# Low key rows of the scores: a transfer from the rounded rows in place of a cast on Vector

## The chip, the cores and the metric

The kernel runs on one core of one Trainium2 chip. Its engines are TensorE (PE, with its weight loads shown apart as PEld), VectorE (DVE), ScalarE (ACT), GpSimd (POOL) and SyncE (SP), which here only issues transfers. The metric is the device time of one execution in microseconds. Three runs of the kernel before took 872.01, 875.14 and 871.11 us, a median of 872.01.

## The reference, cut to what matters

Causal attention with a forget bias, then a channel mix; batch 8, 8 heads, 576 positions, head size 64, model width 512, hidden width 1024.

```python
scores = scale * np.matmul(q, k.transpose(0, 1, 3, 2))
cum = np.cumsum(np.maximum(s, 0.0), axis=-1)
bias = -(cum[:, :, :, None] - cum[:, :, None, :])
scores = np.where(causal, -1e9, scores + np.minimum(bias, 0.0))
attn = softmax(scores)
x = (attn @ v)                       # heads side by side: B, S, 512
x_prev = x shifted by one position
xk = mu_k * x + (1 - mu_k) * x_prev
xr = mu_r * x + (1 - mu_r) * x_prev
k = np.maximum(xk @ w_k, 0.0)
out = sigmoid(xr @ w_r) * (k * k @ w_v)
```

## The kernel before

Attention goes in 36 visits, each of one batch and one pair of heads; a visit of batch 0 covers part of the query tiles (three tiles, later the other two), a visit of batches 1 to 7 all five. After the output of enough positions is there, a chunk of 256 positions goes through the channel mix (18 chunks: hidden layer L1184, gate L1226, output L1251). The work of chunks is laid between the visits, and the last chunks stand alone at the end.

Products of two float32 matrices are made of rounded halves (the type fp32r, which TensorE reads in one pass): high part times high part, and so on. For the scores of the last 32 visits, `split_qk` prepares this, head by head (j = 0, 1, so 64 times). The raw keys of a pair lie in `raw`, head 0 on partitions 0 to 63 and head 1 on 64 to 127. ACT rounds the own half into `KH` (L693). POOL subtracts, and writes what rounding left into the other half of `KH` (L697). ACT rounds the queries into `G` (L708), POOL writes their rest into `QL` (L712). A score is then two matmuls into one PSUM bank (L761): `KH` with `G` over 128 rows, and `KL` with `QL` over 67 rows. Rows 0 to 63 of `KL` are the rounded keys once more, on low partitions for both heads; rows 64 to 66 are three parts of the prefix sums, which a small transfer brings (L687). Before the change, rows 0 to 63 were written by a cast on DVE (L703) from the same raw keys. `KH`, `KL`, `G` and `QL` have three buffers each.

The order on every engine is written by a planner (`Plan`). Each operation is added as a task with an engine, a duration from a formula, its readers and writers, and a due time. The planner runs a list schedule forward with these durations, derives new due times backward, does this 20 times and emits the order that ended first by its own reckoning. A task's `quarters` (the partitions of input and output) make an engine 20 ns later when they differ from those of the task before. So a task that changes its engine or its formula changes the order of everything. Every engine works through its list in order; SP issues transfers one after the other, and one whose source or target isn't ready holds those behind it.

Operations that matter here: on DVE the reduction of scores with the mask (L779), the rest of the turned weights `pl` (L889), which the matmuls with the values wait for (L1019), the channel mix's `xp` (L1130), `xl` (L1156), squares (L1206) and `kl` (L1213); on ACT the exponentials (L797) and the casts `ph` (L885); on POOL the normalization (L813) and the rest of the values (L632); on SP the loads of queries (L658), keys (L645), values (L621) and of a chunk's positions `x` (L1276).

Of the kernel before, what the change touches and what calls it, by code (L numbers as in the profile page):

```python
# [29 lines left out]
def f32(ap):  # L30
    return ap.bitcast(F32)
# [281 lines left out]
def forgetting_attention_then_channel_mix(  # L313
# [16 lines left out]
    nc = tc.nc  # L330

    B, H, D, S = q.shape
# [20 lines left out]
    def sbuf(shape, tag, bufs=1, dtype=F32):  # L353
        return plan.buffer(sb, shape, dtype, tag, bufs)
# [15 lines left out]
    def at_quarters(i, quarters):  # L370
        if quarters != (0, 0):
            plan.quarters[i] = quarters
        return i

    def act(emit, reads, writes, n, extra=51, table=0, quarters=(0, 0)):
        return at_quarters(
            plan.add("ACT", n * 0.8333 + extra, emit, reads, writes, land=table), quarters
        )

    def dve(emit, reads, writes, n, rate=0.96, extra=70, quarters=(0, 0)):  # L380
        return at_quarters(plan.add("DVE", n / rate + extra, emit, reads, writes), quarters)

    def pool(emit, reads, writes, n, extra, rate=0.8333, quarters=(0, 0)):
        return at_quarters(plan.add("POOL", n * rate + extra, emit, reads, writes), quarters)

    def dma(emit, reads, writes, ns):
        return plan.add("SP", 1.286 * ns, emit, reads, writes, land=1300)
# [279 lines left out]
    def ahead(emit, what, n):  # L667
        due, plan.due = plan.due, -2.0e5
        dve(emit, [], [what], n)
        plan.due = due  # L670

    def split_qk(b, hp, qs, k):

        nq, nk = qs[0].n, k.n
        found = []
        for j in range(2):
            own, other = slice(64 * j, 64 * j + 64), slice(64 - 64 * j, P - 64 * j)  # L680
            QQ, K = (sbuf([P, n], x, 3, F32R) for n, x in ((nq, "G"), (nk, "KH")))
            QL, KB = (sbuf([P, S], x, 3, F32R) for x in ("QL", "KL"))
            if made[0] < 3:
                made[0] += 1
                ahead(lambda QL=QL: nc.vector.memset(f32(QL.get()[64:67]), 1.0), (QL, 1), S)
            dma(
                lambda j=j, KB=KB: nc.sync.dma_start(  # L687
                    f32(KB.get()[64:67, 0:nk]), cum3_d.ap[b * H + 2 * hp + j, :, 0:nk]
                ),
                [(cum3_d, i) for i in range(3)], [(KB, 1)], 40,  # L690
            )
            act(
                lambda own=own, K=K: nc.scalar.copy(K.get()[own], k.get()[own]),  # L693
                [(k, j)], [(K, j)], nk, 90,
            )
            pool(
                lambda own=own, other=other, K=K: nc.gpsimd.tensor_tensor(  # L697
                    out=K.get()[other], in0=k.get()[own], in1=f32(K.get()[own]), op=ALU.subtract
                ),
                [(k, j), (K, j)], [(K, 1 - j)], nk, 210, 2.21, (2 * j, 2 - 2 * j),  # L700
            )
            dve(
                lambda own=own, KB=KB: nc.vector.tensor_copy(KB.get()[0:64, 0:nk], k.get()[own]),  # L703
                [(k, j)], [(KB, 0)], nk, 1.92, 150, (2 * j, 0),
            )
            x = qs[j]
            act(
                lambda x=x, QQ=QQ: nc.scalar.copy(QQ.get(), x.get()),  # L708
                [(x, 0), (x, 1)], [(QQ, 0), (QQ, 1)], nq, 90,
            )  # L710
            pool(
                lambda x=x, QQ=QQ, QL=QL: nc.gpsimd.tensor_tensor(  # L712
                    out=QL.get()[0:64, 0:nq], in0=x.get()[0:64], in1=f32(QQ.get()[0:64]),
                    op=ALU.subtract,
                ),
                [(x, 0), (QQ, 0)], [(QL, 0)], nq, 210, 2.21,
            )
            found.append(((QQ, K, P), (QL, KB, 67)))
        return found
# [632 lines left out]
    def prepare(n):  # L1352
        qs, ks = loaded.pop(n)
        b, hp, tiles = visits[n]
        vn = load_values(b, hp, -(-KN[tiles[-1]] // P), n < PLAIN)
        QKs[n] = [[(x, ks)] for x in qs] if n < PLAINQ else split_qk(b, hp, qs, ks)
        Vs[n] = vn if n < PLAIN else split_v(vn, vn.n // P)
# [119 lines left out]
```

## Time and profile before

| | |
|---|---|
| median of three runs | 872.01 us |
| the profiled execution, its own time | 871.47 us |
| its span | 869.7 us |
| granted TensorE clock | full (0.999 of 2.4 GHz) |
| busy: PE, DVE, ACT, POOL | 851.7, 698.5, 688.4, 449.5 us |

Busy PE counts a matmul from its start to the modelled end, and neighbours overlap, so a busy share of 98% does not say that TensorE streams without pause. The chain of waits follows the work that ended last back from the end; it says which engine was waited for, and there PE has 76%.

### The profile page before, as it was taken

The numbers are of one execution on the slowest core, as the hardware profiler recorded it, in microseconds if no ns is written. First come the engines' busy times: TensorE is split into PE (matmuls) and PEld (weight loads), VectorE is DVE, ScalarE is ACT, GpSimd is POOL, SyncE is SP. The second block draws the span as 40 slices with busy tenths as digits, with TensorE's granted clock in tenths as the row PEclk, the third lists the DMA queues.
The fourth block names the chain that finished last, engine by engine and source line by source line (L and its number), as shares of the span: only waits on it lengthen the run. The fifth ranks groups of instructions, "written<-read, shape, count | busy, mean of one in ns | idle before, by whom it ended". The sixth has DMA issues, their size and how long they took to land.

```text
span 869.7 us, 17512 instructions
## 1 busy us (share of the span) xinstructions
PE 851.7 (98%) x5519; PEld 751.0 (86%) x5519; DVE 698.5 (80%) x2143; ACT 688.4 (79%) x1854; POOL 449.5 (52%) x719
## 2 busy tenths in 40 slices
PE   9999999999999999999999999999999999999998
PEld 8778789789888888989898988898988889888986
DVE  8999789889888998789878888888888888555431
ACT  6999999999978987898979787988887978445331
POOL 5877887884754665455646545445653642000000
PEclk9999999999999999999999999999999999999999
DMA  8775233251332323223322313132412110100100
GB/s 248 254 233 154 86 115 109 85 153 47 109 117 67 120 64 110 67 83 93 89 88 72 109 55 120 58 104 72 122 55 92 44 62 16 57 22 34 49 25 24
DMA packets 48125, 80.10 MB, mean 92 GB/s; under 512 B 8160, under 2 KB 21472, under 8 KB 48032
## 3 DMA queue, kind: packets, MB, share of 16 engines
q1 hardware_dynamic: 48032, 78.99, 29.7%
q8 instruction: 43, 0.70, 0.3%
q14 instruction: 50, 0.41, 0.2%
HBM read 59.64 MB, written 19.33 MB: 91 GB/s over the span
## 4 chain that ended last, share of the span: by engine, by line
PE 76%; DVE 12%; ACT 8%; issue 3%; DMA 1%; SPq 0%; POOL 0%; ACTq 0%; DVEq 0%
PE m L1251 16%; PE m L1184 16%; PE m L1226 9%; PE s L761 8%; PE po L1019 7%; PE t L856 7%; DVE W L779 3%; ACT W L797 3%; DVE KL L703 2%; DVE pl L889 2%; PE t L1251 2%; PE po L1005 2%; PE s L1184 2%; PE t L1184 2%; PE s L750 1%
## 5 line engine op out<-in xcount | busy, mean ns | idle before, releaser
L1184 PE MATMUL m<-xh,w_k 128*128 128x256 f32 x976 | 205.5, 288 | 0.5 <-ACT xh L1152 0.3
L797 ACT ACTIVATE W<-W,nm 64x64 f32<-64x64 f32 (+4 forms) x320 | 179.6, 562 | 26.3 <-DVE nm L779 22.0
L1251 PE MATMUL m<-w_v,kh 128*128 128x512 f32 x528 | 187.6, 406 | 0.0
L813 POOL TENSOR_SCALAR W<-W,rinv 128x192 f32<-128x192 f32 (+4 forms) x320 | 166.7, 540 | 25.4 <-DVE rinv L839 23.8
L1184 PEld LDWEIGHTS m<-xh,w_k 128*128 128x128 f32 x976 | 160.2, 189 | 3.0 <-ACT xh L1152 0.7
L779 DVE CUSTOM_DVE_ANT_0 W<-s,lower 128x448 f32<-128x448 f32 (+5 forms) x320 | 130.1, 414 | 26.2 <-PE s L761 21.0
L1184 PE MATMUL m<-xl,w_k 128*128 128x256 f32 x488 | 138.9, 285 | 0.0
L856 PE MATMUL t<-ident,W 128*128 128x128 f32 (+1 forms) x736 | 134.0, 275 | 4.5 <-DVE xT L1057 1.8
L697 POOL TENSOR_TENSOR KH<-raw,KH 64x576 fp32r<-64x576 f32 x64 | 92.9, 1451 | 83.9 <-ACT KH L693 45.5
L889 DVE TENSOR_TENSOR pl<-t,ph 128x512 fp32r<-128x512 f32 x224 | 106.4, 484 | 11.9 <-ACT ph L885 9.9
L856 PEld LDWEIGHTS t<-ident,W 128*128 128x128 f32 (+1 forms) x736 | 89.5, 137 | 25.7 <-DVE xT L1057 2.8
L1251 PEld LDWEIGHTS m<-w_v,kh 128*128 128x128 f32 x528 | 97.9, 189 | 14.3 <-ACT g L1238 0.3
L761 PE MATMUL s<-KH,G 128*64 128x64 f32 (+1 forms) x360 | 108.7, 309 | 0.5 <-DVE nm L779 0.5
L885 ACT CAST ph<-t 128x512 fp32r<-128x512 f32 x224 | 93.2, 424 | 17.4 <-PE t L856 14.6
L761 PE MATMUL s<-KL,QL 67*64 67x64 f32 (+1 forms) x360 | 106.1, 299 | 0.0
L1251 PE MATMUL m<-w_v,kl 128*128 128x512 f32 x264 | 106.0, 402 | 0.0
L1130 DVE SCALAR_TENSOR_TENSOR xp<-x,mu,xp 128x256 f32<-128x256 f32 (+3 forms) x184 | 76.3, 415 | 26.5 <-ACT xp L1123 24.1
L1226 PE MATMUL m<-w_r,xh 128*128 128x512 f32 x264 | 95.1, 406 | 0.5 <-DVE kl L1213 0.5
L1123 ACT ACTIVATE xp<-x,mu 128x256 f32<-128x256 f32 (+3 forms) x184 | 77.6, 422 | 22.3 <-DMA x<-x_d 11.7
L712 POOL TENSOR_TENSOR QL<-raw,G 64x576 fp32r<-64x576 f32 (+1 forms) x64 | 86.6, 1353 | 13.3 <-ACT G L708 11.2
L1184 PEld LDWEIGHTS m<-xl,w_k 128*128 128x128 f32 x488 | 92.4, 189 | 0.9
L632 POOL TENSOR_TENSOR V<-vn,V 128x320 fp32r<-128x320 f32 x56 | 48.4, 882 | 70.9 <-ACT V L628 64.5
(161 smaller groups left out, 1899.6 us busy)
## 6 DMA issues: line engine op xcount, KB each, us to landing
raw<-in_q SPq DMA_DIRECT2D x112, 144.0 KB
raw<-in_k SPq DMA_DIRECT2D x32, 288.0 KB
out<-g SPq DMA_DIRECT2D x36, 256.0 KB
vn<-in_v SPq DMA_DIRECT2D x28, 320.0 KB
x_d<-xT SPq DMA_DIRECT2D x28, 288.5 KB
x<-x_d SPq DMA_DIRECT2D x11, 514.0 KB
w_k<-in_moe_w_k SPq DMA_DIRECT2D x8, 512.0 KB
w_v<-in_moe_w_v SPq DMA_DIRECT2D x8, 512.0 KB
```

The costliest lines, as they stand in the source:

```text
L697: lambda own=own, other=other, K=K: nc.gpsimd.tensor_tensor(out=K.get()[other], in0=k.get()[own], in1=f32(K.get()[own]), op=ALU.subtract),
L712: lambda x=x, QQ=QQ, QL=QL: nc.gpsimd.tensor_tensor(out=QL.get()[0:64, 0:nq], in0=x.get()[0:64], in1=f32(QQ.get()[0:64]), op=ALU.subtract,),
L761: lambda x=x, G=G, K=K, n=n: nc.tensor.matmul(ps.get()[:m, :w], G.get()[:n, q0 : q0 + m], K.get()[:n, k0 : k0 + w], start=x == 0, stop=x == 1,
L779: lambda a=a, e=e, to=to, i=i: nc.vector.tensor_tensor_reduce(out=W.ap[:m, to : to + e - a], in0=ps.get()[:m, a - k0 : e - k0], in1=lower. ...
L797: lambda: nc.scalar.activation(W.ap[:m, :n], W.ap[:m, :n], AF.Exp, bias=nm.get()[:m, 3 * t + mi : 3 * t + mi + 1], scale=-1.0, accum_out=s ...
L813: lambda: nc.gpsimd.tensor_scalar(out=to.ap[:m, c : c + n], in0=W.ap[:m, :n], scalar1=rinv.get()[:m, t : t + 1], scalar2=1.0, op0=ALU.mult ...
L856: lambda: nc.tensor.transpose(ps.get()[0:m, place : place + P], pt[t].ap[:, k0 + front(t, tiles) : k0 + front(t, tiles) + m], ident.ap,),
L885: act(lambda: nc.scalar.copy(strips(ph), src()), [ps], [(ph, k) for k in ks], n * m)
L889: lambda: nc.vector.tensor_tensor(out=strips(pl), in0=src(), in1=f32(strips(ph)), op=ALU.subtract),
L1184: lambda u=u, f=f, c=c, n=n, w=w, x=x: nc.tensor.matmul(ps.get()[:, u * CT : (u + 1) * CT], weight["k", c, f // 4].get()[:, w, f % 4 * P : ...
L1226: lambda c=c, n=n, x=x, w=w: nc.tensor.matmul(ps.get(), x.get()[:, c, ts], weight["r", c, 0].get()[:, w], start=c == 0 and n == 0, stop=c ...
L1251: lambda f=f, n=n, x=x, w=w: nc.tensor.matmul(ps.get(), x.get()[:, f, ts], weight["v", f, 0].get()[:, w], start=f == 0 and n == 0, stop=f ...
```

## The change

The cast on DVE of rows 0 to 63 of `KL` is taken out. A transfer on SP's queue writes them, from the own half of `KH`, once ACT has rounded it. The values are the same. The ACT cast's task also tells the planner its partitions now (`quarters`). Nothing else differs, but the planner's order does. Lines behind the change move down by two.

```diff
             act(
                 lambda own=own, K=K: nc.scalar.copy(K.get()[own], k.get()[own]),
-                [(k, j)], [(K, j)], nk, 90,
+                [(k, j)], [(K, j)], nk, 90, quarters=(2 * j, 2 * j),
             )
...
-            dve(
-                lambda own=own, KB=KB: nc.vector.tensor_copy(KB.get()[0:64, 0:nk], k.get()[own]),
-                [(k, j)], [(KB, 0)], nk, 1.92, 150, (2 * j, 0),
+            dma(
+                lambda own=own, K=K, KB=KB: nc.sync.dma_start(
+                    f32(KB.get()[0:64, 0:nk]), f32(K.get()[own])
+                ),
+                [(K, j)], [(KB, 0)], 410 * nk / S,
             )
```

What stands on DVE of the kernel before around the 35th of the 64 casts (a name's number tells its buffer apart; `W` and `nm` are scores and their maxima):

```order
L1130 SCALAR_TENSOR_TENSOR xp_307<-x_164,mu_75,xp_307 128x256
L779 ISA W_71,nm_229<-s_143,lower 64x64
L779 ISA nm_229 64x1
L703 CAST KL_633<-raw_389 64x576
L889 TENSOR_TENSOR pl<-t_316,ph_1439 128x384
L889 TENSOR_TENSOR pl<-t_310,ph_1439 128x256
L1156 TENSOR_TENSOR xl_897<-xp_307,xh_882 128x512
L889 TENSOR_TENSOR pl<-t_310,ph_1439 128x128
L839 RECIPROCAL rinv_313<-rinv_313 128x5
```

And on DVE of the changed kernel at the same scores:

```order
L1132 SCALAR_TENSOR_TENSOR xp_309<-x_164,mu_75,xp_309 128x256
L891 TENSOR_TENSOR pl<-t_315,ph_1436 128x384
L781 ISA W_71,nm_229<-s_143,lower 64x64
L781 ISA nm_229 64x1
L1132 SCALAR_TENSOR_TENSOR xp_309<-x_164,mu_75,xp_309 128x256
L891 TENSOR_TENSOR pl<-t_307,ph_1436 128x256
L841 RECIPROCAL rinv_312<-rinv_312 128x5
L1158 TENSOR_TENSOR xl_926<-xp_309,xh_915 128x512
L891 TENSOR_TENSOR pl<-t_307,ph_1436 128x128
```

The cast that stood ahead of two writes of `pl` is gone, and the first `pl` stands ahead of the reduction.

SP's queue in the kernel before, from the load of a chunk's positions in the third batch on:

```order
L1276 DMA x_164<-x_d_79 128x4x193
L687 DMA KL_569<-cum_d 3x576
L658 DMA raw_433<-in_q 64x576 x2
L658 DMA raw_357<-in_q 64x576 x2
L621 DMA vn_100<-in_v 128x640
L1268 DMA out<-g_1208 128x512
L645 DMA raw_94<-in_k 128x576
L687 DMA KL_633<-cum_d 3x576
```

And in the changed kernel from the same load:

```order
L1278 DMA x_164<-x_d_79 128x4x193
L658 DMA raw_401<-in_q 64x576 x2
L687 DMA KL_527<-cum_d 3x576
L1270 DMA out<-g_1129 128x512
L703 DMA KL_661<-KH_680 64x576
L658 DMA raw_428<-in_q 64x576 x2
L687 DMA KL_585<-cum_d 3x576
L1399 DMA x_d_80<-xT_195 128x577
L621 DMA vn_100<-in_v 128x640
L703 DMA KL_527<-KH_532 64x576
```

Each head has one more entry (L703) between the loads, and the loads behind it issue after it.

## Rows read from the trace of the kernel before

**Rows 1.** The page: busy shares, and the chain of waits by engine and line.

```profile
PE 851.7 (98%) x5519; PEld 751.0 (86%) x5519; DVE 698.5 (80%) x2143; ACT 688.4 (79%) x1854; POOL 449.5 (52%) x719
...
PE 76%; DVE 12%; ACT 8%; issue 3%; DMA 1%; SPq 0%; POOL 0%; ACTq 0%; DVEq 0%
PE m L1251 16%; PE m L1184 16%; PE m L1226 9%; PE s L761 8%; PE po L1019 7%; PE t L856 7%; DVE W L779 3%; ACT W L797 3%; DVE KL L703 2%; DVE pl L889 2%; PE t L1251 2%; PE po L1005 2%; PE s L1184 2%; PE t L1184 2%; PE s L750 1%
```

**Rows 2.** Busy time by stage: stretch, its length, each engine, clock, DMA share.

```profile
0.00:50.00 50.00, 45.26 (x318) 38.45 (x319) 46.38 (x129) 41.95 (x132) 37.77 (x84) 1.00 0.81 245
50.00:250.00 200.00, 194.39 (x1268) 168.42 (x1268) 181.24 (x532) 187.77 (x506) 154.13 (x227) 1.00 0.39 120
250.00:700.00 450.00, 446.06 (x2933) 397.59 (x2931) 381.06 (x1273) 379.56 (x1035) 244.69 (x382) 1.00 0.28 84
750.00:869.70 119.70, 115.97 (x687) 101.83 (x685) 49.63 (x86) 43.37 (x84) 0.00 (x0) 0.99 0.10 33
```

**Rows 3.** The chain of waits by line, of 50 to 250, then 250 to 700.

```profile
by line: PE m L1184 11.4%; PE t L856 8.4%; PE s L761 7.3%; ACT W L797 6.7%; issue 6.5%; PE m L1251 6.4%; PE m L1226 5.5%; PE po L1005 5.0%; DVE W L779 4.6%; DVE KL L703 4.6%; DVE pl L889 3.9%; PE po L1019 3.9%; ACT xp L1123 3.3%; ACT ph L88
...
by line: PE m L1184 20.3%; PE m L1251 18.2%; PE m L1226 11.3%; PE s L761 11.0%; PE po L1019 10.2%; PE t L856 7.2%; DVE W L779 3.0%; DVE KL L703 2.3%; DVE pl L889 2.1%; issue 2.0%; ACT W L797 1.5%; PE t L956 1.3%; PE t L1019 1.2%; DVE pl L94
```

**Rows 4.** Groups by form, the cast: count, busy us, mean ns, idle before.

```profile
L703 DVE CAST KL<-raw 64x576 fp32r<-64x576 f32 x64 | 50.1, 784 | 1.0
```

**Rows 5.** Single lines: minimum, median, maximum ns, first and last start.

```profile
L703 DVE CAST KL<-raw x64: 417/518/2062, 33.5 to 698.3; 64x576 fp32r<-64x576 f32 x64
...
L697 POOL TENSOR_TENSOR KH<-raw,KH x64: 1405/1428/1708, 32.6 to 695.2; 64x576 fp32r<-64x576 f32 x64
```

**Rows 6.** Timeline, a cast with POOL idle (start, us, instruction).

```profile
59.94 0.46 DVE L703 CAST KL<-raw 64x576 fp32r<-64x576 f32 x1
...
60.49 1.41 POOL L697 TENSOR_TENSOR KH<-raw,KH 64x576 fp32r<-64x576 f32 x1 [1.04 <-issue]
```

**Rows 7.** Timeline from 339 to 343, a cast with POOL at work.

```profile
339.55 1.71 POOL L632 TENSOR_TENSOR V<-vn,V 128x320 fp32r<-128x320 f32 x2 [6.13 <-ACT V L628]
...
340.55 1.02 DVE L703 CAST KL<-raw 64x576 fp32r<-64x576 f32 x1
...
341.34 1.52 POOL L697 TENSOR_TENSOR KH<-raw,KH 64x576 fp32r<-64x576 f32 x1
...
341.50 0.97 DVE L889 TENSOR_TENSOR pl<-t,ph 128x384 fp32r<-128x384 f32 x2
...
342.09 0.13 PEld L1019 LDWEIGHTS po<-pl,V 128*64 128x64 f32 x1 [0.46 <-DVE pl L889]
```

**Rows 8.** Timeline, the rounding of keys and their head's first score.

```profile
156.70 0.67 ACT L693 CAST KH<-raw 64x576 fp32r<-64x576 f32 x1
...
161.76 0.24 PE L761 MATMUL s<-KH,G 128*64 128x64 f32 x1
...
694.37 0.67 ACT L693 CAST KH<-raw 64x576 fp32r<-64x576 f32 x1
...
722.79 0.22 PE L761 MATMUL s<-KH,G 128*64 128x64 f32 x1
```

**Rows 9.** The chain in order of time: a transfer of keys at the start.

```profile
3.66 4.36 DMA KH<-in_k
```

**Rows 10.** Waits: who waited for whom, us in total, times, longest.

```profile
SPq L687 <- PE s L761: 141.9, 44, 10.6
...
ACT xp L1123 <- DMA x<-x_d: 11.7, 6, 4.8
```

**Rows 11.** SP's issues by line: minimum, median, maximum ns, first and last start.

```profile
L658 SPq DMA_DIRECT2D raw<-in_q x128: 465/476/1580, 14.4 to 661.4; - x128
...
L1276 SPq DMA_DIRECT2D x<-x_d x23: 529/564/582, 107.0 to 803.8; - x23
```

**Rows 12.** The page: the DMA queue's packets, MB, share of 16 engines.

```profile
q1 hardware_dynamic: 48032, 78.99, 29.7%
```

## The prediction

> **What bounds the kernel now.** I read four views: the page for the engines and the chain of waits, then busy time by stage, then the chain of the two middle stages, then single instructions around the cast.
>
> The page shows PE at 98% and DVE and ACT near 80% [rows 1]. Busy PE includes overlaps, so I go by the chain: 76% PE, 12% DVE, 8% ACT. So for about a fifth of the span TensorE waits for something DVE or ACT has not finished. The cast, L703, has 2% of the chain by itself, about 17 us.
>
> By stage [rows 2] there are three cases. Up to 50 us the DMA engines are 0.81 busy with the first weights. From 50 to 250 us DVE is busy 181.24 of 200 and ACT 187.77, so both are nearly full and PE waits for both. From 250 to 700 us DVE has 381.06 and ACT 379.56 of 450, and PE is close to its own pace. From 750 us on TensorE works alone on the last chunks, POOL does nothing, and no cast is left (the last starts at 698.3 [rows 5]). The clock is full throughout, so it is no term.
>
> In the chain of the stages [rows 3] the cast has 4.6% of the 200 us, which is 9.2 us, and 2.3% of the 450 us, which is 10.35 us: 19.6 us together, against 17 by the page's rounded share.
>
> **What a cast costs.** The 64 casts are busy 50.1 us, 784 ns each in the mean [rows 4], but 417 at least, 518 in the middle and 2062 at most [rows 5]. Their form is one and the same, so something else stretches them. With POOL idle a cast takes 0.46 us [rows 6]. In the worked case [rows 7] POOL works on two subtractions from 339.55 to 341.26; the cast starts at 340.55 and ends at 341.57, 0.31 us after POOL was done. POOL's next instruction, the key subtraction, then takes 1.52 us where its median is 1.43 [rows 5]. So the cast waits for POOL and POOL waits for the cast. All 64 at 0.455 would be 29.1 us; the other 21 us are such waits.
>
> The Trainium skill (SBUF — State Buffer, section "Who interferes with whom") calls the port pair that VectorE's two-port copies share with GpSimd an exclusive lock: the second to start is blocked until the first is done. The times of rows 7 agree. By that rule the 21 us go with the cast. If the two engines shared bandwidth instead, as the same page's section "A bandwidth-pool intuition that's wrong" describes and rejects, other DVE work would go on being stretched and only 29.1 of the 50.1 us would go.
>
> **Removed.** DVE loses 64 instructions and 50.1 us. What that is worth is what the chain loses, between 0 (something else is late at the same moment) and 19.6 us (all of the cast's share). The worked case gives the fraction: behind the 1.02 us cast stand two writes of `pl`, and TensorE's weight load of the matmul that needs them waits 0.46 us for `pl` [rows 7]. 0.46 of 1.02 is 0.45. I take 0.45 of 19.6 = 8.8 us. What is late next, in 50 to 250 us, is ACT: it has only 12.2 of 200 us idle [rows 2], and its work is not made less. In 250 to 700 us it is TensorE's own pace and the chain from scores over L779 to the exponentials. The order of DVE shows the place: the first write of `pl` now stands ahead of the reduction, with nothing between it and the `xp` before.
>
> **Added.** 64 transfers of 64 rows of 2304 bytes, 147 KB each, 9.4 MB in all. The queue moved 78.99 MB in 29.7% of the engines' time [rows 12], so at the same rate they add 3.5 points; only before 50 us are the DMA engines near full [rows 2], and few transfers fall there. On SP an issue of a load of the same shape takes 0.476 us [rows 11], 30 us in all on a queue that mostly waits: the prefix-sum rows alone wait 141.9 us for TensorE to release `KL` [rows 10].
>
> A new wait: a score can start when ACT has rounded the keys, SP has come to the transfer, and it has landed. No landing of such a transfer is shown. The nearest is the load of 160 KB of keys at the start, 4.36 us [rows 9]. POOL's half of the same `KH` buffer is needed too, and takes 1.43 us after the same rounding, so the path grows by at most 2.9 us where POOL starts at once. Against it stands the lead from rounding to first score, which I paired head by head: 64 roundings against the first scores of 64 heads in order. The tightest but one is 161.76 less 157.37 = 4.4 us in the stage up to 250 us; at the last head it is 722.79 less 695.04 = 27.8 us [rows 8]. After 260 us nearly all leads lie above 15 us. So the transfer is hidden: 0 of cost. If the cover is gone, the first heads would each pay up to 2.9 us, for the 16 of batch 0 and the next visits 46 us at the very most, which the planner can see and order around.
>
> What stands behind the new transfer in SP's list are the loads of queries, values and `x`. It waits for ACT's rounding, so these can issue later than before; their users are ACT's casts and the `xp` work. I take 0, and price the other end below.
>
> **Moved.** ACT's and POOL's counts stay. The planner's order changes everywhere, in the start too. No row prices that; the nearest is PE's idle time up to 50 us, 4.7 us [rows 2], which a new order could halve or double. I take 0 and keep 4.7 to either side.
>
> **Sum.** 871.47 (the profiled execution, 1.8 over its span) − 8.8 + 0 + 0 = 862.7. That execution lay 0.5 below the median of 872.01, so the forecast in those terms is 863.2 us.
>
> **Rivals.** *All of the chain's share goes*, because POOL is freed as well and the rest of the chain is not late: 871.5 − 19.6 + 0.5 = 852.4. For it: the casts block both engines. Against: ACT's idle 12.2 us of 200.
>
> *Something else is late anyway.* ACT takes DVE's place up to 250 us and nothing is gained there; later 0.45 of 10.35 = 4.7, less 0.9 us for a transfer or two that is late: 871.5 − 3.8 + 0.5 = 868.2. For it: ACT is busier than DVE there.
>
> *SP's queue falls behind, slower than before.* The new transfers wait for ACT while loads of `x` stand behind them. Now ACT waits for `x` 6 times, 11.7 us [rows 10], 1.95 us each, at 23 loads [rows 11]. If the other 17 come as late, ACT loses 33.2 us, and by the fraction of 0.45 the end moves by 14.9: 871.5 − 8.8 + 14.9 + 0.5 = 878.1. It decides from the point where ACT's wait for `x` grows by more than about 20 us in total. Against: SP's list is issued well ahead, and 23 loads spread over 700 us.
>
> *The change does not do what it says*: the stretch is shared bandwidth and stays on other work. Then 29.1/50.1 of 8.8 is 5.1 and the time 866.9. Against: the cast of rows 7 ends just behind POOL, and one with POOL idle is not stretched.
>
> **How the numbers follow.** A measurement of this kernel can tell about 0.5% from no change, here 4.4 us: faster is below 867.6, slower above 876.4. Chances: the forecast 0.54, the full share 0.10, something else late 0.22, SP behind 0.12, shared bandwidth 0.02. So faster is 0.54 + 0.10 + 0.02 = 0.66, same 0.22, slower 0.12. The forecast's own range, with the new order's 4.7 either way, is 858 to 868. The range that holds 8 in 10 reaches over the case of 868.2 with the same 4.7 and to the full share: 852 to 876.
>
> **What would show it.** Right: no cast on DVE, DVE's busy time down by about 50 us, POOL's key subtraction down to near its minimum of 1.41, the chain's DVE share below 10%, and PE's weight loads waiting less for `pl`. The KL matmul starts right behind the KH matmul, not microseconds later. Wrong: TensorE or its weight loads waiting for a transfer into `KL`; ACT waiting for `x` or for the loads of queries clearly above 11.7 us; the chain in 50 to 250 us filled by ACT to the same length; or a start that reaches 50 us's work later than before.

## The result, and the profile after

The changed kernel takes 864.27 us in the median of four runs (862.82 to 865.54), against 872.14 beside it; the ratio is 0.9904 with a 95% interval of 0.9875 to 0.9933. The forecast was 863.2, range 852 to 876. The profiled execution, the slowest of the four, took 865.54 us over a span of 863.8.

The page of the kernel after, busy shares, the DMA queue and the chain of waits, answers to [rows 1] and [rows 12]:

```profile
PE 848.6 (98%) x5510; PEld 752.3 (87%) x5510; DVE 656.0 (76%) x2079; ACT 687.8 (80%) x1854; POOL 444.1 (51%) x719
...
q1 hardware_dynamic: 53152, 88.43, 34.9%
...
PE 87%; ACT 5%; DVE 3%; DMA 3%; issue 1%; SPq 0%; POOL 0%; ACTq 0%; DVEq 0%; POOLq 0%
PE m L1253 19%; PE m L1186 18%; PE m L1228 10%; PE s L763 9%; PE po L1021 8%; PE t L858 8%; PE po L1007 3%; DMA x<-x_d 3%; PE t L1253 2%; PE t L1186 2%; PE s L1186 2%; ACT W L799 1%; PE s L741 1%; PE s L752 1%; PE t L1021 1%
```

DVE's 64 casts are gone and 42.5 us of its busy time (the prediction said about 50; the casts' rows overlap their neighbours). More telling is the chain: DVE falls from 12% to 3%, PE rises from 76% to 87%, and a new name stands in it, the landing of `x`, 3%. The transfers add 9.4 MB, and the share of time that the queue's packets take rises by 5.2 points, where the prediction had 3.5.

Busy time by stage, with the columns of [rows 2]:

```profile
0.00:50.00 50.00, 45.46 (x306) 39.12 (x307) 43.27 (x123) 40.97 (x128) 36.63 (x83) 0.98 0.80 238
50.00:250.00 200.00, 196.76 (x1289) 171.63 (x1288) 166.66 (x516) 188.77 (x510) 152.56 (x228) 1.00 0.50 143
250.00:700.00 450.00, 446.36 (x2944) 400.10 (x2943) 361.44 (x1248) 383.06 (x1047) 245.81 (x389) 1.00 0.33 96
```

From 50 to 250 us TensorE starts 1289 matmuls where it started 1268, from 250 to 700 us 2944 against 2933. Up to 50 us it starts 306 against 318, at a mean clock of 0.98. But 9 of these 12 are idle matmuls on the identity with which the planner fills gaps (62 in all against 71), and a second profile of the same kernel (e6) has 314 up to 50 us, at full clock. So the middle is better, and the start is not shown to be worse.

The chain of the two middle stages, answering to [rows 3]:

```profile
by line: PE m L1253 16.4%; PE m L1186 15.4%; PE t L858 13.2%; PE s L763 12.2%; PE po L1021 9.0%; PE m L1228 8.6%; PE po L1007 7.9%; issue 2.4%; ACT W L799 2.1%; DVE W L781 2.0%; ACT ph L887 1.5%; PE t L1021 1.2%; DVE pl L891 1.1%; DVE xp L1
...
by line: PE m L1186 21.9%; PE m L1253 19.3%; PE m L1228 11.7%; PE s L763 11.4%; PE po L1021 10.6%; PE t L858 7.9%; DMA x<-x_d 4.9%; ACT W L799 1.5%; PE t L958 1.4%; PE t L1021 1.2%; issue 1.1%; DVE W L781 0.9%; ACT KH L693 0.8%; ACT xp L112
```

With the cast gone, `pl` behind it (3.9% and 2.1% before) shrinks as well; the exponentials fall from 6.7% to 2.1% in the first of the two stages. The 4.9% of `x` are those of one execution: the second profile of the kernel has 3.4% there, and the new order without the transfers (e4) still 2.4%.

Single lines of after (minimum, median, maximum ns), POOL's key subtraction and the new transfer's issue:

```profile
L697 POOL TENSOR_TENSOR KH<-raw,KH x64: 1399/1425/1443, 33.0 to 689.3; 64x576 fp32r<-64x576 f32 x64
L703 SPq DMA_DIRECT2D KL<-KH x64: 467/490/1007, 31.8 to 689.2; - x64
```

POOL's maximum drops from 1708 [rows 5] to 1443 ns: none of the 64 is held up any more. Who waits for whom, us in total, times, longest, a line of before and then two of after:

```profile
PEld po L1019 <- DVE pl L889: 7.2, 12, 1.3
```

```profile
ACT xp L1125 <- DMA x<-x_d: 14.4, 7, 4.0
...
PEld po L1021 <- DVE pl L891: 0.5, 2, 0.3
```

The weight loads of the value matmuls wait 0.5 us for `pl` in all, where they waited 7.2. ACT waits 14.4 us for `x`, where it waited 11.7 [rows 10]. No matmul and no weight load of after waits for a transfer.

### The profile page after: what moved, and what is told of

Read it like the earlier page. It is cut to its first block, busy times and chain, and to the rows that moved or that the text cites. A ratio compares the mean times of both kernels' runs of the same rounds, so it can differ in the third digit from the quotient of the medians.

```text
span 863.8 us, 17613 instructions
## 1 busy us (share of the span) xinstructions
PE 848.6 (98%) x5510; PEld 752.3 (87%) x5510; DVE 656.0 (76%) x2079; ACT 687.8 (80%) x1854; POOL 444.1 (51%) x719
## 4 chain that ended last, share of the span: by engine, by line
PE 87%; ACT 5%; DVE 3%; DMA 3%; issue 1%; SPq 0%; POOL 0%; ACTq 0%; DVEq 0%; POOLq 0%
PE m L1253 19%; PE m L1186 18%; PE m L1228 10%; PE s L763 9%; PE po L1021 8%; PE t L858 8%; PE po L1007 3%; DMA x<-x_d 3%; PE t L1253 2%; PE t L1186 2%; PE s L1186 2%; ACT W L799 1%; PE s L741 1%; PE s L752 1%; PE t L1021 1%
## 5 line engine op out<-in xcount | busy, mean ns | idle before, releaser
L1186 PE MATMUL m<-xh,w_k 128*128 128x256 f32 x976 | 200.3, 286 | 0.0
L799 ACT ACTIVATE W<-W,nm 128x448 f32<-128x448 f32 (+4 forms) x320 | 179.5, 562 | 22.9 <-DVE nm L781 18.7
L815 POOL TENSOR_SCALAR W<-W,rinv 128x448 f32<-128x448 f32 (+4 forms) x320 | 165.2, 535 | 20.5 <-DVE rinv L841 15.8
L697 POOL TENSOR_TENSOR KH<-raw,KH 64x576 fp32r<-64x576 f32 x64 | 91.1, 1424 | 72.4 <-issue 25.8
L763 PE MATMUL s<-KL,QL 67*64 67x64 f32 (+2 forms) x360 | 105.8, 300 | 0.0
L887 ACT CAST ph<-t 128x512 fp32r<-128x512 f32 x224 | 93.3, 424 | 13.6 <-PE t L858 10.3
L1125 ACT ACTIVATE xp<-x,mu 128x256 f32<-128x256 f32 (+3 forms) x184 | 77.5, 421 | 24.7 <-DMA x<-x_d 14.4
L1021 PE MATMUL po<-ph,V 128*128 128x448 f32 x280 | 82.9, 323 | 2.6 <-ACT ph L887 2.5
```

The source lines that it names most:

```text
L697: lambda own=own, other=other, K=K: nc.gpsimd.tensor_tensor(out=K.get()[other], in0=k.get()[own], in1=f32(K.get()[own]), op=ALU.subtract),
L763: lambda x=x, G=G, K=K, n=n: nc.tensor.matmul(ps.get()[:m, :w], G.get()[:n, q0 : q0 + m], K.get()[:n, k0 : k0 + w], start=x == 0, stop=x == 1,
L799: lambda: nc.scalar.activation(W.ap[:m, :n], W.ap[:m, :n], AF.Exp, bias=nm.get()[:m, 3 * t + mi : 3 * t + mi + 1], scale=-1.0, accum_out=s ...
L815: lambda: nc.gpsimd.tensor_scalar(out=to.ap[:m, c : c + n], in0=W.ap[:m, :n], scalar1=rinv.get()[:m, t : t + 1], scalar2=1.0, op0=ALU.mult ...
L887: act(lambda: nc.scalar.copy(strips(ph), src()), [ps], [(ph, k) for k in ks], n * m)
L1021: lambda: nc.tensor.matmul(po.get()[: P if both else 64, at + q0 - base : at + q0 - base + m], V.get()[:, kb, 2 * j : 2 * j + (2 if both e ...
```

## The experiments

Each run below the first row was timed beside the kernel before once more, and its ratio is to those times. "Old order" means that PE, ACT, DVE and POOL run the list of the kernel before, but for what the edit puts in the cast's place; "new order" that of after. The edits are shown shortened.

| run | order | low key rows by | median us | ratio to before | 95% interval |
|---|---|---|---|---|---|
| after | new | transfer | 864.27 | 0.9904 | 0.9875 to 0.9933 |
| e6_after_again | new | transfer | 863.49 | 0.9897 | 0.9879 to 0.9915 |
| e1_old_order_transfer | old | transfer | 868.32 | 0.9965 | 0.9952 to 0.9977 |
| e2_new_order_cast | new | copy on DVE | 905.74 | 1.0400 | 1.0386 to 1.0414 |
| e3_old_order_none | old | left out (61 of 64) | 860.76 | 0.9879 | 0.9865 to 0.9892 |
| e4_new_order_none | new | left out (61 of 64) | 863.19 | 0.9911 | 0.9897 to 0.9924 |
| e5_old_order_memset | old | a fill of DVE, 0.455 us | 860.85 | 0.9866 | 0.9848 to 0.9883 |
| f1_reduce | old | one-pass move on DVE | 863.92 | 0.9908 | 0.9895 to 0.9922 |
| f3_hybrid | old | cast for 8 heads, then transfer | 865.51 | 0.9927 | 0.9914 to 0.9941 |
| e7_idle_longer | planned anew | transfer | 863.13 | 0.9894 | 0.9876 to 0.9912 |
| e8_act_queue | new | transfer from ACT's queue | 868.77 | 0.9960 | 0.9945 to 0.9974 |
| e10_quarters | planned anew | cast | 875.10 | 1.0034 | 1.0022 to 1.0047 |
| e9_idle_early_x | planned anew | transfer | 860.46 | 0.9875 | 0.9857 to 0.9892 |

**The two halves of the change apart.** Old order with the transfer:

```diff
-  lambda own=own, KB=KB: nc.vector.tensor_copy(KB.get()[0:64, 0:nk], k.get()[own]),
+  lambda own=own, K=K, KB=KB, both=both: both(own, K, KB),      # ACT's rounding calls it too
...
+  def both(own, K, KB):
+      calls.append(None)
+      if len(calls) == 2:
+          nc.sync.dma_start(f32(KB.get()[0:64, 0:nk]), f32(K.get()[own]))
```

> The order of before on PE, ACT, DVE and POOL is kept to the instruction; the 64 casts on DVE are taken out, and 64 transfers from the rounded rows are issued on SP, at the cast's place in the plan or right behind ACT's rounding where that comes later. Theory (the cast on DVE and its waits with POOL cost the time, the new order nothing): 863 to 866 us, as after. Rival (the new order made the gain): 870 to 874, as before. Rival (the transfer's waits on SP cost as much as the cast in an order not planned for them): over 874.

0.9965: the theory and both rivals are off. The transfer alone gains 0.35%, about a third of what the change does. New order with a copy on DVE:

```diff
-  nc.sync.dma_start(f32(KB.get()[0:64, 0:nk]), f32(K.get()[own]))
+  nc.vector.tensor_copy(KB.get()[0:64, 0:nk], K.get()[own])
```

> The order of after on PE, ACT and POOL is kept; the transfer is taken out and DVE copies the rounded rows at the transfer's place in the plan, 64 copies of the cast's form. Theory: 871 to 875 us, as before or a little above, since this order leaves DVE no room for the copies, and the copies are again stretched by POOL (about 50 us busy). Rival (new order): 864 to 867.

905.74, far above either. So the new order with a copy on DVE in it makes no gain; what the order is worth by itself is told by the runs without cast and transfer, below. The size had not been expected. The copies by minimum, median and maximum:

```profile
L703 DVE CAST KL<-KH x64: 442/1156/2589, 32.3 to 728.1; 64x576 fp32r<-64x576 f32 x64
```

One of them in the timeline, and POOL's subtraction of the same moment:

```profile
308.17 1.60 DVE L703 CAST KL<-KH 64x576 fp32r<-64x576 f32 x1
...
308.02 1.44 POOL L697 TENSOR_TENSOR KH<-raw,KH 64x576 fp32r<-64x576 f32 x1 [2.70 <-ACT KH L693]
```

This copy reads `KH`, so it can start when ACT has rounded, and so can POOL's subtraction. POOL goes first at 308.02, ends at 309.46, and the copy ends 0.31 us later. The median of 518 ns becomes 1156. But these copies also stand where the plan left DVE no room, so the 42 us by which the run lies above after are not parted further.

**The worth of the cast.** Old order, cast left out:

```diff
-  lambda own=own, KB=KB: nc.vector.tensor_copy(KB.get()[0:64, 0:nk], k.get()[own]),
+  lambda own=own, KB=KB: (
+      casts.append(None),
+      len(casts) <= 3 and nc.vector.tensor_copy(KB.get()[0:64, 0:nk], k.get()[own]),
+  ),
```

> The order of before; 61 of the 64 casts are left out and nothing takes their place (the low key rows keep what the first three wrote). It gives the whole worth of the cast in the old order. Theory: 862 to 866 us, equal to the run with transfers in the old order within 2 us, since transfers are hidden. Rival (transfers cost on SP): 3 us or more below that run. Rival (new order): 870 to 874.

860.76, 10.6 us below before: more than the theory's range, and 7.6 us below the same order with transfers, so here the rival on SP is right. Busy time by stage, beside [rows 2]:

```profile
50.00:250.00 200.00, 198.32 (x1308) 173.33 (x1308) 167.08 (x520) 190.75 (x516) 151.36 (x227) 1.00 0.40 122
250.00:700.00 450.00, 449.34 (x2955) 402.44 (x2954) 363.43 (x1255) 383.19 (x1051) 246.34 (x394) 1.00 0.27 84
```

ACT goes from 187.77 to 190.75 of 200 in the first of the two stages. TensorE starts 40 more matmuls than before there and 22 more in the second, but a count in a fixed window says little of time, as the two windows hold different matmuls. TensorE's list is the same in both kernels, so the same matmul can be looked for in both (before, then this run):

```profile
0.00:250.00 250.00, 239.65 (x1585) 206.88 (x1586) 227.62 (x660) 229.72 (x637) 191.90 (x310) 1.00 0.48 145
```

```profile
0.00:244.90 244.90, 238.64 (x1585) 206.95 (x1586) 210.15 (x637) 229.32 (x637) 188.25 (x310) 1.00 0.48 148
```

The 1585th matmul, at 250 us in before, comes 5.1 us earlier, and the 4515th, at 700 us, comes 11.1 us earlier (at 688.9). So 46% of the gain lies before 250 us.

New order, transfers left out in the same way:

> The order of after; 61 of the 64 transfers are left out (the low key rows keep what the first three wrote). It gives what the transfers cost in the new order. Theory: 862.5 to 864.5 us, within 2 us of after. Rival (a transfer that holds SP's queue makes loads of x late, which stand in the chain of after with 5% of 250 to 700 us): 858 to 861, and ACT's wait for x falls from 14.4 us to below 8.

863.19, a ratio of 0.9911 where the changed kernel itself has 0.9904 and 0.9897. The transfers cost nothing that can be measured in the new order. ACT's wait for `x` is 11.0 us here, not below 8 as that rival asked. The new order as such is 0.32% behind the old one (0.9911 against 0.9879), some 2.8 us. In the two profiles, by the columns that TensorE has worked through (idle matmuls left out), it is 4.1 us behind at 165 us and 3.2 at the end, so the loss has arisen by 165 us; its cause is open.

**DVE time or waits.** The cast in the old order replaced by a fill of the same length without a source:

```diff
-  nc.vector.tensor_copy(KB.get()[0:64, 0:nk], k.get()[own])
+  nc.vector.memset(f32(KB.get()[0:64, 0:476]), 0.0)        # from the 4th head on
```

> The order of before; in place of 61 of the 64 casts DVE fills 476 of the 576 columns with zeros, about as long as a cast that nothing holds up (0.45 us by the fills of 320 and 576 columns in the trace of before, 0.325 and 0.538), from no source (the low key rows are wrong). It parts the 10.6 us that leaving the casts out saved into DVE time and waits with POOL. Theory (the waits of cast and POOL for each other are the larger part): 863 to 866 us, and no fill over 0.6 us. Rival (DVE time of any kind costs that much): 869 to 872.

The fills by minimum, median and maximum:

```profile
L708 DVE MEMSET KL<- x61: 455/455/455, 56.2 to 687.8; 64x476 f32 x61
```

860.85: the same as with nothing there, and below what the theory asked for. 28 us of DVE time, in the cast's place and of its unhindered length, cost nothing. Every fill takes 455 ns, and 48 of the 61 ran while POOL was at work; of the casts of before, the 12 that POOL left alone took 441 to 456 ns and the others up to 2062. So of the 10.6 us the waits of cast and POOL for each other are all that shows, DVE's part of them and POOL's together (POOL's busy time falls from 449.5 to 442.6 us). The next run keeps the computation whole and moves the rows by another instruction:

```diff
-  nc.vector.tensor_copy(KB.get()[0:64, 0:nk], k.get()[own])
+  nc.vector.tensor_reduce(out=KB.get()[0:64, 0:nk],
+      in_=k.get()[own].rearrange("p (x o) -> p x o", o=1), axis=X, op=max)
```

> The order of before, nothing left out; the 64 casts on DVE are written as a maximum over groups of one element, which moves and rounds the same rows in one pass but is another instruction. Theory (the cast costs time only because it and POOL wait for each other, and this form does not join in that): every instance near 0.66 us (576 columns at the rate of DVE's other one-pass work), 42 us of DVE in all, and 860 to 864 us, though DVE is as busy as with unhindered casts and more. Rival (DVE reading from SBUF while POOL works is held up in any form): instances up to 2 us and 869 to 874 us.

The group by form (count, busy us, mean ns), then the spread of it and of POOL's key subtraction:

```profile
L703 DVE TENSOR_REDUCE KL<-raw 64x576 fp32r<-64x576 f32 x64 | 47.5, 742 | 1.0
```

```profile
L703 DVE TENSOR_REDUCE KL<-raw x64: 703/747/749, 33.6 to 690.7; 64x576 fp32r<-64x576 f32 x64
...
L697 POOL TENSOR_TENSOR KH<-raw,KH x64: 1397/1426/1437, 32.8 to 687.5; 64x576 fp32r<-64x576 f32 x64
```

47.5 us of DVE against the cast's 50.1 [rows 4], the same order on every engine, the same rows read: and 863.92 us, 0.9908. Without a transfer and with almost the same busy DVE it gains what the change gains. It stays about 3 us behind the run with nothing there; its instances are longer than the fills (742 against 455 ns), and whether that or the reading costs it is not parted. The rival (any form is held up) falls: 53 of the 64 ran beside POOL, and no instance exceeds 749 ns. The Trainium skill (SBUF — State Buffer, "Who interferes with whom") says that VectorE contends with GpSimd in its two-port copies and, where GpSimd reads SBUF, with two inputs from SBUF, and not with one input or none in other modes; the three forms agree: the cast up to 2062 ns, the fill 455 and the reduction 749 at most.

**What the transfer costs where no plan makes room.** In the old order with transfers, the third head's transfer is issued on SP, and its first use, a matmul with `KL`, follows after a wait (timeline; the row names another transfer as the releaser, which is inferred, but this one is what the matmul needs):

```profile
49.82 0.49 SPq L686 DMA_DIRECT2D KL<-KH  x1
...
55.49 0.95 PE L775 MATMUL s<-KL,QL 67*128 67x448 f32 x2 [3.30 <-DMA x_d<-w_v]
```

The landing takes at most 5.67 us from the issue; in the trace's record of landings the last of its sixteen parts comes at 55.36. ACT had rounded these keys by 42.44. But the transfer has the cast's place in the old plan, and there the cast ran at 50.88, ending 0.35 us before the matmul. In the new order the same head's transfer is issued 9.2 us before its first use (after):

```profile
43.38 0.49 SPq L703 DMA_DIRECT2D KL<-KH  x1
...
52.60 0.69 PE L763 MATMUL s<-KL,QL 67*128 67x448 f32 x2
```

The old order with transfers by stage (columns as in [rows 2]):

```profile
52.00:54.00 2.00, 0.20 (x2) 0.00 (x0) 1.59 (x5) 1.36 (x3) 1.48 (x2) 0.99 1.06 305
54.00:60.80 6.80, 5.31 (x17) 4.54 (x17) 2.29 (x6) 3.43 (x8) 3.49 (x4) 0.50 0.49 152
```

The queues are full here (305 GB/s, share 1.06), TensorE is busy 0.20 of 2 us, and then the granted clock is 0.50, the lower level of 1.2 GHz, for 6.8 us. The 451st matmul, at 70.0 us with nothing in the cast's place, comes at 75.4 here: this one place is 5.4 of the 8.0 us between the two profiled executions (858.6 and 866.6). Keeping the cast for the first 8 heads avoids it:

```diff
+  cast = heads[0] < 8
+  heads[0] += 1
...
+  if cast:
+      nc.vector.tensor_copy(KB.get()[0:64, 0:nk], k.get()[own])
```

> The order of before; the first 8 heads keep the cast on DVE, the other 56 get the transfer at the cast's place. Theory (of the 7.6 us by which transfers in the old order lie over leaving them out, most is one landing of 5.6 us near 50 us, while the first weights fill the queues, with TensorE waiting 3.3 us and then 6.8 us at half clock): 861 to 864 us, full clock near 50 us. Rival (each transfer costs a little on SP's queue all along): 867 to 869, as with 64 transfers.

865.51, between theory and rival. 0.0038 of 0.0086 between all transfers and none come back, 3.3 us. The clock is full near 50 us, as expected. The rest has a place too. Up to 245 us the run keeps up with the one that leaves the casts out (1585 matmuls by 245.1 against 244.9), so neither the 8 casts nor the transfers until then cost anything that shows. Then, here and in the run without casts (e3):

```profile
242.50 0.49 SPq L697 DMA_DIRECT2D KL<-KH  x1
...
244.68 0.56 SPq L1299 DMA_DIRECT2D x<-x_d  x1
...
248.88 0.77 ACT L1146 ACTIVATE xp<-x,mu 128x128 f32<-128x128 f32 x2 [4.05 <-DMA x<-x_d]
```

```profile
242.84 0.56 SPq L1280 DMA_DIRECT2D x<-x_d  x1
```

The load of `x` stands behind the transfer and issues 1.84 us later than without it. ACT waits 4.05 us for `x`, against 1.7. TensorE then runs dry, and the clock falls (here, then e3):

```profile
250.00:253.00 3.00, 1.75 (x8) 1.75 (x9) 2.42 (x8) 2.50 (x8) 0.00 (x0) 0.71 0.00 0
```

```profile
250.00:253.00 3.00, 3.00 (x28) 3.00 (x27) 1.77 (x9) 2.95 (x9) 1.81 (x2) 1.00 0.19 51
```

The 1667th matmul comes at 258.8 against 254.9: these 14 us hold 3.7 of the 3.9 us between the two profiled executions. The old order with all transfers loses 2.3 us at the same place, also with 4.0 us of waiting for `x`. So in the old order the transfers cost at two places, one landing and one late load of `x`, and not a little each.

**The start of the new order.** In after the clock falls too (first two rows); with more idle matmuls it does not (third, a run in which the planner filled gaps for longer):

```profile
46.00:48.00 2.00, 0.83 (x3) 0.38 (x3) 2.00 (x7) 2.00 (x7) 1.83 (x4) 0.99 0.82 279
48.00:51.40 3.40, 3.40 (x12) 2.92 (x13) 3.18 (x7) 3.19 (x8) 3.23 (x5) 0.50 0.38 106
```

```profile
48.00:51.40 3.40, 3.40 (x28) 2.83 (x27) 3.25 (x7) 3.24 (x10) 2.73 (x4) 1.00 0.56 136
```

```diff
-  if plan.busy_from is None:  plan.busy_from = y
+  passed.append(y)
+  if len(passed) == 49:  plan.busy_from = y
```

> The changed kernel, but the planner fills TensorE's gaps with idle matmuls on the identity until the scores of the second batch begin (the 49th rounded product) and not only to the first rounded product; the order after that is planned anew. Theory (the 3.4 us at half clock near 48 us, after a stretch in which TensorE idled, cost the new order about 2 us at the start): full clock throughout, 861 to 863 us. Rival (the start is bound by loads and DVE, not by the clock): 864 to 866.

Full clock, 863.13 against 863.49: no difference. The theory that the half clock cost the new order its 2 us is not borne out; this run's order differs too.

**The queue.**

```diff
-  nc.sync.dma_start(f32(KB.get()[0:64, 0:nk]), f32(K.get()[own]))
+  nc.scalar.dma_start(f32(KB.get()[0:64, 0:nk]), f32(K.get()[own]))
```

> The changed kernel with the 64 transfers issued from ACT's queue instead of SP's, at the same place in the plan. It takes the waits on ACT's rounding out of SP's queue. Theory (SP's queue holds nothing that matters, ACT is nearly full up to 250 us): 864 to 870 us, no faster. Rival (SP's queue behind): 859 to 862, and ACT's wait for x below 10 us against 14.4.

The issues on ACT's queue, ACT's wait for `x`, and the stretch near 53 us (columns as in [rows 2]):

```profile
L703 ACTq DMA_DIRECT2D KL<-KH x64: 468/468/505, 31.6 to 694.3; - x64
```

```profile
ACT xp L1125 <- DMA x<-x_d: 12.6, 6, 3.8
```

```profile
52.70:63.00 10.30, 9.74 (x36) 7.88 (x35) 6.35 (x19) 7.38 (x18) 7.60 (x9) 0.50 0.68 218
```

868.77, slower than after, as the theory had it: 64 issues take 30 us on ACT's queue, and the wait for `x` hardly falls. Near 53 us the clock is at half for 10.3 us in this execution, but that is not the reason: another of the seven ran at full clock and took 869.82 us.

**The other part alone.**

```diff
-  [(k, j)], [(K, j)], nk, 90,
+  [(k, j)], [(K, j)], nk, 90, quarters=(2 * j, 2 * j),
```

> The kernel before with the one other part of the change alone: ACT's rounding tells the planner its partitions. The cast stays on DVE, and the order is planned anew. Theory (this part is worth nothing but a new order): 868 to 875 us. Rival (it carries the gain): 863 to 866.

875.10, slower than before by 0.34%: just outside the theory's range, and opposite to the rival. No work is added or removed (the planner sets 4 idle matmuls fewer, 5515 against 5519 in all), so this is what a new order alone can do.

**A version that beats before and after.** In after SP's list shows why `x` is late near 655 us (SP, then ACT):

```profile
654.60 0.54 SPq L703 DMA_DIRECT2D KL<-KH  x1
655.23 0.56 SPq L1278 DMA_DIRECT2D x<-x_d  x1
...
653.92 0.66 ACT L693 CAST KH<-raw 64x576 fp32r<-64x576 f32 x1
...
660.17 0.78 ACT L1125 ACTIVATE xp<-x,mu 128x128 f32<-128x128 f32 x2 [2.66 <-DMA x<-x_d]
```

The transfer waits for the rounding that ends at 654.58, the load of `x` issues behind it, and ACT waits 2.66 us for `x`.

```diff
-  [(x, i)], 5.7 * n,
+  [(x, i)], 5.7 * n + 1500,        # and the longer run of idle matmuls
```

> The changed kernel with the longer run of idle matmuls and, besides, 1.5 us (before the planner's factor of 1.286) added to what the planner counts for a load of x, so that it sets these loads and what they wait for earlier; planned anew. In the chain of after the landings of x stand with 4.9% of 250 to 700 us, 22 us. Theory (with the cast's waits gone, late loads of x are the next thing that holds ACT): 858 to 862 us, and ACT's wait for x under 8 us. Rival (the other chains are as late, and a new order moves the time by 3 us either way, as the partitions alone did): 862 to 867.

ACT's wait for `x`, and the chain by line from 250 to 700 us:

```profile
ACT xp L1127 <- DMA x<-x_d: 7.4, 2, 3.9
```

```profile
by line: PE m L1255 24.6%; PE m L1188 23.4%; PE s L764 13.0%; PE m L1230 12.5%; PE po L1023 11.8%; PE t L860 9.3%; PE t L960 1.7%; PE t L1023 1.4%; DVE W L783 0.5%; issue 0.3%; ACT W L801 0.3%; DVE pl L947 0.3%; DVE xp L1134 0.2%; DVE pl L8
```

860.46 us, 0.9875, the best of the complete versions. From the chain of 250 to 700 us the landing of `x` is gone, and nearly all of it is TensorE. Its four runs (859.91 to 861.22) lie below those of after beside before (862.79 to 864.37), but the two were not timed together and their intervals overlap a little. That the loads of `x` are the reason is in line with the chain; a new order alone moved the time by as much.

## Why the prediction was right

*What bounds it*: right. The cast's waits stood in the chain, and DVE's share fell below 10% as said.

*Removed, 8.8 us*: the right mechanism, mis-sized downward. Leaving the cast out in the old order gives 10.6 us, 0.54 of the chain's 19.6 and not 0.45. The fraction came from one cast of 64, so that it lay so near is luck in part. The prediction opened the term with 50.1 us that DVE loses; the runs show that 28 us of them, in pieces of the cast's unhindered length, are free, and that the waits with POOL are what costs. The split by stage was right: 4.1 of 8.8 us before 250 us by the chain's shares, 47%, and 5.1 of 11.1 measured, 46%. ACT, named as late next there, did not take the gain away: its idle time shrank from 12.2 to 9.25 us.

*The transfer, 0*: right for the new order (0.9911 without, 0.9904 and 0.9897 with), wrong for the old, where it costs 7.6 us: some 5.4 by one landing near 50 us and 2.3 by one late load of `x` near 250 us. The 4.36 us taken for a landing was too low: it took 5.54. The lead was reckoned from ACT's rounding, but the transfer starts where it stands in SP's list, which was 7.4 us later for that head. The new order issues that head's transfer 9.2 us before its first use; that it does so for all heads because the planner knows the transfer is argued, and in line with no matmul waiting for one.

*The new order, 0 within 4.7*: it costs 2.8 us (0.9911 against 0.9879), within the bound. Why stays open; a run without the half clock at the start, in one more order, was no faster.

The sum by the measured terms is −10.6 + 2.8 + 0 = −7.8, and −7.9 was measured between the medians. That the forecast of −8.8 lies so close is luck: two errors, too little for the cast and nothing for the order, partly cancel.

*The rivals*: the full chain's share is refuted by leaving the cast out (10.6 of 19.6). SP falling behind is there in small: ACT's wait for `x` grew from 11.7 to 14.4 us, far from the 20 us more that would have decided; in the old order one late load by itself cost 2 to 4 us. Shared bandwidth is refuted by the reduction in the cast's place, which was never stretched.

## What to carry to other kernels

When instances of one form differ widely in time, look at what another engine does in that moment before counting the engine's busy time: here 50 us of casts cost 10.6 us by their waits, while nearly as much DVE time in another form cost about 3 and the unhindered length nothing. Where the waits are the cost, an instruction that doesn't join in them, in the same place, gained here as much as moving the work away. A transfer put in the place of a cast needs an earlier place: here it took 5.5 us from issue to landing where the cast took 0.44, and it held a load behind it. When a planner orders the work, measure the edit in the old order and the new order without the edit; a new order alone moved this kernel by 0.3%. While the order stays the same, look for the same matmul in both traces: that shows where time is lost, which counts in fixed windows do not.

## What the runs showed of the hardware

A form that moves the rows in one pass on DVE was never held up while POOL worked (747 ns in the median, 749 at most), although its unhindered time is longer than the cast's. A transfer of 147 KB from SBUF to SBUF took 5.54 us from issue to landing while the queues were full (305 GB/s). An issue of such a transfer took 0.49 us on SP's queue and 0.47 on ACT's in the median. TensorE's granted clock fell from 2.4 to 1.2 GHz after TensorE had been busy 0.83 of 2 us (after) and 0.20 of 2 us (old order with transfers), for 3.4 and 6.8 us, and with casts for 8 heads after it had waited 2.1 us, near 251 us. After a wait of 2.0 us in the old order with transfers, near 255 us, it did not fall.
